# The sinks' products written first into the values' banks, and another order of work from step 7 on

## The chip, the cores and the metric

The kernel runs on one core of one Trainium2 chip. The metric is the device time of one launch in microseconds. Lower is better.

## What is computed

Attention over a window with sinks, and then a gated block. `q`, `k` and `v` have 4 batches, 8 heads, 768 positions and 64 features; a query sees the 4 first positions (the sinks) and the 128 positions that end at itself. The second part works on the heads put side by side (`x`: 4 x 768 x 512). Cut to what matters:

```
scores = scale * np.matmul(q, k.transpose(0, 1, 3, 2))
keep = is_sink | in_window                  # pos < 4, or 0 <= rel < 128
scores = np.where(keep, scores, -1000000000.0)
a = np.exp(scores - max); a = a / (np.sum(a) + 1e-09)
x = np.matmul(a, v)                         # then heads side by side
...
for k in range(5):                          # a causal convolution of 5 taps
    gate_pre += conv_w[k][None, None, :] * xp[:, k:k + S, :]
gate = 1.0 / (1.0 + np.exp(-gate_pre))
val = x @ w_val
out = gate * val @ w_out
```

All values are float32.

## The kernel before

**Steps and blocks.** The attention is cut into 24 steps: 4 batches, 3 parts of 256 positions, and 2 quads of 4 heads. Two steps (both quads of one part) make one of 12 blocks of the gated part. No loop runs on the chip: everything is laid out in one written order, the text `ORDER`. Its tokens are a short name and a step or block number, and each calls one function. Every engine, and each DMA queue, runs its own instructions in the order in which the tokens call them; semaphores hold an instruction until its inputs are there and its output's place is free.

**Tokens of a step (s is the step).** `kq.s` and `vv.s` load keys, queries and values through SP's queue. `s0.s` and `s1.s` are the scores of two halves of the quad (TensorE, L395), followed by a copy under a mask and a maximum on VectorE (L400, L404 or L409). `e0.s`, `e1.s` are the exponentials (ScalarE, L420), `rec.s` the reciprocal of the sums (L426, L427), `norm.s` the products with it on GpSimd (L435 to L443). `tx.s` turns the probabilities with sixteen transposes on TensorE (L455); `px.s` (VectorE, L486) and `py.s` (ScalarE, L494) take them out of PSUM, under the two masks. `sk.s` turns the sinks' probabilities (one transpose, L463), `ts.s` takes them out (L473). `vl.s` (`values`, L513) multiplies the turned probabilities with the values, 48 records in a step and 32 in a step of a batch's first part; `si.s` (`sinks`, L521) adds the sinks' part with two products. `sv.s` prepares the sinks' values (L260 on ScalarE, L263 twice on GpSimd).

**What follows a step.** The result of `vl` and `si` lies in the tile `xv`, two banks of PSUM, of which there is one copy. `xc.s` (L528) and `xh.s` (L536) copy it out on ScalarE, `hd.s` (L540) writes the four columns ahead of it for the convolution, `xl.s` (L544) and `c4.s` (L549) work on the copies on GpSimd, and `c0.s` and `c1.s` (L557, four instructions each on VectorE) read `xv` for the other four taps. The next step may write into `xv` only when all of them have read.

**Tokens of a block (m is the block).** `th` is the gate's tanh. `v0.m` to `v3.m` (L576) are the products with `w_val`, twelve matmuls each; `g0`, `g1` (L595) the gate on VectorE, `h0`, `h1` (L601) and `l0`, `l1` (L605) the split into a high and a low part on ScalarE and GpSimd; `o0.m` to `o3.m` (L629, in the last half L625) the products with `w_out`; `t0`, `t1` (L648, L638) take them out, `d0`, `d1` store them through SP's queue.

**Places in PSUM.** `pr` is two pairs of banks, which scores and transposes take in turn; `ac` (the list `homes`) is two single banks, taken by `sk`, by `v0` and `v2`, and by `o0` and `o2`, and put back by `ts`, by `g` and by `t`. `xv` is the last two.

**Forms of TensorE's array.** The products use four tilings of the array, shown in the profile as rows by columns: `128*128` (`v`, `o`, `sk`), `64*32` (`s`), `64*64` (`vl`) and `64*128` (`tx`, `si`).

Of the kernel before, what the change touches and what calls it, by code (L numbers as in the profile page):

```python
# [56 lines left out]
py.11 px.11 norm.12 xl.9 vv.13 vl.10 si.10 xc.10 hd.10 xh.10 kq.14 d1.3 tx.12 py.12 px.12 c4.10 c0.10 warm_up
v0.4 xl.10 v1.4 g0.4 d1.1 h0.4 l0.4 vv.11 c1.10 th.9 v2.4 e1.13 v3.4 g1.4 sk.11 ts.11 s1.14 s0.14 h1.4 vl.11
si.11 o0.4 sk.12 ts.12 e0.13 rec.13 l1.4 xc.11 hd.11 c4.11 sv.13 e0.14 norm.13 c0.11 o1.4 kq.18 e1.14 t0.4
c1.11 kq.15 o2.4 d0.3 o3.4 s0.18 s0.15 vv.12 th.11 xh.11 sv.12 vl.12 si.12 t1.4 xc.12 tx.13 rec.14 hd.12 xl.11  # L60
v0.5 c4.12 norm.14 xh.12 e0.15 px.13 c0.12 c1.12 v2.5 xl.12 v3.5 g1.5 py.13 th.10 v1.5 g0.5 h0.5 sk.13 ts.13
s1.15 h1.5 s1.18 d0.4 e1.15 vl.13 l0.5 si.13 o0.5 l1.5 xc.13 rec.15 hd.13 xh.13 s0.16 e0.16 th.12 tx.14 px.14
o2.5 kq.17 o1.5 t0.5 py.14 c4.13 c0.13 o3.5 t1.5 vv.14 e0.18 xl.13 vv.18 c1.13 s1.16 d1.5 sk.14 ts.14 norm.15
sk.15 ts.15 sv.18 vl.14 si.14 xc.14 hd.14 tx.15 px.15 e1.16 c4.14 c0.14 rec.16 py.15 norm.16 e1.18 c1.14 xh.14
v0.6 v1.6 g0.6 v2.6 h0.6 s0.17 vv.15 kq.19 s0.19 vl.15 si.15 rec.18 l0.6 th.13 vv.16 e0.17 xc.15 v3.6 g1.6
xl.14 c4.15 s1.17 hd.15 s1.19 th.14 h1.6 sk.16 ts.16 l1.6 xh.15 c0.15 xl.15 e1.17 rec.17 kq.20 e0.19 o0.6 o1.6
t0.6 tx.16 py.16 c1.15 px.16 v0.7 v1.7 norm.18 sk.18 ts.18 s0.20 d1.4 kq.21 e1.19 d0.6 vl.16 v2.7 e0.20 g0.7
h0.7 norm.17 l0.7 si.16 xc.16 c4.16 hd.16 tx.18 px.18 py.18 tx.17 v3.7 px.17 c0.16 o2.6 o3.6 th.15 g1.7 vv.23
rec.19 xh.16 c1.16 py.17 t1.6 s1.20 h1.7 xl.16 s0.21 e1.20 sk.17 ts.17 norm.19 o0.7 vv.17 th.16 rec.20 d0.5
l1.7 vl.17 si.17 xc.17 c4.17 hd.17 xh.17 e0.21 xl.17 norm.20 d1.6 c0.17 tx.19 py.19 o2.7 o3.7 o1.7 t0.7 c1.17  # L70
th.17 px.19 t1.7 kq.23 d1.7 s1.21 vl.18 d0.7 si.18 xc.18 c4.18 hd.18 vv.19 xh.18 e1.21 sv.19 tx.20 vv.20 px.20
c0.18 v2.8 xl.18 v3.8 g1.8 h1.8 kq.22 c1.18 th.18 v0.8 v1.8 sk.19 py.20 ts.19 g0.8 h0.8 vl.19 si.19 s1.22 l1.8
rec.21 s0.22 xc.19 hd.19 l0.8 xh.19 c4.19 xl.19 sk.20 o0.8 ts.20 o1.8 c0.19 c1.19 norm.21 e1.22 t0.8 d0.8 o2.8
e0.22 rec.22 v0.9 norm.22 th.19 tx.21 px.21 py.21 vl.20 si.20 vv.21 xc.20 c4.20 hd.20 xh.20 xl.20 s1.23 e1.23
s0.23 vv.22 v1.9 g0.9 h0.9 o3.8 t1.8 v2.9 e0.23 v3.9 l0.9 c0.20 c1.20 rec.23 sk.21 norm.23 ts.21 vl.21 si.21
xc.21 c4.21 g1.9 h1.9 l1.9 tx.22 py.22 px.22 tx.23 py.23 hd.21 xh.21 o2.9 xl.21 o0.9 o3.9 c0.21 o1.9 t1.9 t0.9
c1.21 px.23 th.20 sk.22 ts.22 vl.22 si.22 xc.22 c4.22 xh.22 xl.22 sk.23 ts.23 d1.9 hd.22 c0.22 c1.22 v0.10
v2.10 v1.10 th.22 g0.10 v3.10 h0.10 l0.10 vl.23 si.23 xc.23 c4.23 hd.23 xh.23 xl.23 th.21 flag g1.10 o0.10
o2.10 d1.8 c0.23 c1.23 v0.11 v1.11 th.23 g0.11 h0.11 l0.11 v2.11 d0.9 v3.11 g1.11 o0.11 h1.10 l1.10 h1.11
o1.10 l1.11 o1.11 t0.10 d0.10 t0.11 o3.10 t1.10 o2.11 d1.10 d0.11 o3.11 t1.11  # L80
# [809 lines left out]
```

## Time and profile before

| | |
|---|---|
| median of 3 runs | 263.9 us (263.66 to 264.38) |
| the profiled execution | 264.63 us |
| its span, first to last instruction | 262.8 us |
| granted clock of TensorE, mean | 0.997 |
| busy share PE, PEld, DVE, ACT, POOL | 97%, 78%, 78%, 72%, 67% |

PE is TensorE's matmuls, PEld its weight loads, DVE VectorE, ACT ScalarE, POOL GpSimd, SP the queue of DMAs. A busy share is over the whole span. The chain of waits follows the work that ended last back to its start; its pieces lie end to end, so that the length of a piece is what it added to the time.

### The profile page before, as it was taken

How to read it: one execution, taken by the hardware profiler on the slowest of the kernel's cores; microseconds unless marked ns; L12 is line 12 of the kernel's file. 1: busy time of each engine (PE TensorE's matmuls, PEld its weight loads, DVE VectorE, ACT ScalarE, POOL GpSimd, SP SyncE). 2: the span in 40 equal slices, each digit the busy share in tenths (PEclk: the TensorE clock that was granted, in tenths of full speed). 3: DMA queues.
4: the chain of work that ended last, by engine and by line, in shares of the span. 5: the costliest groups of instructions: out<-in, count | busy, mean ns of one | idle time of the engine just before them, and what ended most of it. 6: DMA issues, size and time to landing. Idle time of an engine off the chain costs nothing.

```text
span 262.8 us, 9921 instructions
## 1 busy us (share of the span) xinstructions
PE 253.6 (97%) x3960; PEld 205.5 (78%) x3964; DVE 204.7 (78%) x561; ACT 188.7 (72%) x692; POOL 177.4 (67%) x241
## 2 busy tenths in 40 slices
PE   7899989999999999999999999999999999999993
PEld 2355569779878878889879779889779788888982
DVE  5976999979979879997869698796878659667610
ACT  3899998979887677974796688986676768444231
POOL 6279897778668992878379665894782985933340
PEclk9999999999999999999999999999999999999998
DMA  6999382364323534755250529253407131030013
GB/s 201 379 340 341 113 262 74 109 168 144 106 78 118 183 131 146 218 171 180 63 174 2 161 81 326 78 185 111 142 4 231 68 106 59 2 122 0 2 44 128
DMA packets 27541, 36.45 MB, mean 139 GB/s; under 512 B 2272, under 2 KB 24032, under 8 KB 27488
## 3 DMA queue, kind: packets, MB, share of 16 engines
q1 hardware_dynamic: 26672, 34.96, 41.7%
q10 hardware_dynamic: 816, 0.79, 0.9%
q8 instruction: 33, 0.54, 0.9%
q14 instruction: 20, 0.16, 0.2%
HBM read 29.45 MB, written 6.29 MB: 136 GB/s over the span
## 4 chain that ended last, share of the span: by engine, by line
PE 79%; ACT 9%; POOL 4%; DMA 4%; DVE 1%; issue 1%; POOLq 0%
PE ac L576 24%; PE ac L629 22%; PE xv L513 11%; PE pr L395 9%; PE pr L455 4%; ACT w L420 4%; PE pr L629 3%; PE xv L521 2%; DMA raw<-in_w_val_dram 2%; DMA vs<-in_vsk_dram 2%; POOL xl L544 1%; PE ac L463 1%; POOL gl L605 1%; POOL vh L263 1%; ACT wv_p L140 1%
## 5 line engine op out<-in xcount | busy, mean ns | idle before, releaser
L557 DVE SCALAR_TENSOR_TENSOR sg<-xv,cw,sg 128x256 f32<-128x256 f32 x192 | 77.8, 474 | 3.3 <-POOL sg L549 2.9
L435 POOL TENSOR_TENSOR wx<-w,sm 128x512 f32<-128x512 f32 x48 | 49.2, 1047 | 5.7 <-DVE sm L427 4.0
L420 ACT ACTIVATE w<-pr,ngm 128x132 f32<-128x132 f32 x136 | 48.6, 370 | 1.6
L576 PE MATMUL ac<-xh,wvh 128*128 128x256 f32 x192 | 48.7, 288 | 0.0
L605 POOL TENSOR_TENSOR gl<-sg,gh 128x512 fp32r<-128x512 f32 x24 | 30.8, 1290 | 26.0 <-ACT gh L601 25.8
L576 PE MATMUL ac<-xh,wvl 128*128 128x256 f32 x192 | 47.0, 279 | 0.0
L549 POOL TENSOR_TENSOR sg<-xt,cw 128x512 f32<-128x512 f32 x24 | 25.5, 1063 | 17.9 <-ACT xt L528 16.5
L576 PEld LDWEIGHTS ac<-xh,wvh 128*128 128x128 f32 x192 | 36.2, 189 | 1.7 <-issue 0.5
L576 PEld LDWEIGHTS ac<-xh,wvl 128*128 128x128 f32 x192 | 36.1, 188 | 0.2
L395 PE MATMUL pr<-k,q 64*32 64x168 f32 x1536 | 35.0, 307 | 0.6 <-DVE wt L486 0.2
L513 PEld LDWEIGHTS xv<-wt,v 64*64 64x64 f32 x1024 | 30.3, 133 | 6.1 <-issue 2.6
L513 PE MATMUL xv<-wt,v 64*64 64x192 f32 (+2 forms) x1024 | 34.5, 278 | 0.2 <-ACT wt L494 0.2
L544 POOL TENSOR_TENSOR xl<-xt,xh 128x512 fp32r<-128x512 f32 x24 | 31.0, 1290 | 3.9 <-DVE sm L427 2.5
L629 PE MATMUL ac<-woh,gh 128*128 128x512 f32 x80 | 33.2, 415 | 0.0
L629 PE MATMUL ac<-woh,gl 128*128 128x512 f32 x80 | 31.8, 397 | 0.3 <-POOL gl L605 0.3
L629 PE MATMUL ac<-wol,gh 128*128 128x512 f32 x80 | 31.7, 396 | 0.0
L576 PE MATMUL ac<-xl,wvh 128*128 128x256 f32 x192 | 30.4, 280 | 0.1
L395 PEld LDWEIGHTS pr<-k,q 64*32 64x32 f32 x1536 | 24.0, 106 | 8.1 <-issue 2.1
L400 DVE COPY_PREDICATED pr<-low,pr 128x256 f32<-128x256 uint8 x48 | 20.3, 422 | 9.6 <-PE pr L395 4.9
L420 ACT ACTIVATION_READ_ACCUMULATOR w<-pr,ngm 128x1 f32 x136 | 27.6, 203 | 0.0
L576 PEld LDWEIGHTS ac<-xl,wvh 128*128 128x128 f32 x192 | 25.9, 188 | 0.3 <-POOL xl L544 0.3
L404 DVE TENSOR_REDUCE ngm<-pr 128x4 f32<-128x528 f32 x34 | 24.0, 707 | 1.2
(156 smaller groups left out, 480.0 us busy)
## 6 DMA issues: line engine op xcount, KB each, us to landing
k<-in_kt_dram SPq DMA_DIRECT2D x23, 408.0 KB, 4.1
...
```

Of the source, the lines that this page charges most:

```text
L395: nc.tensor.matmul(ss[e * QB:(e + 1) * QB, j, c * n + x0:c * n + x1], q[js, g, (4 * c + e) * QB:(4 * c + e + 1) * QB], k[js, g, (2 * c + e ...
L400: nc.vector.copy_predicated(sv[:, :, :, :D], low[:, None, None, :].to_broadcast([P, 2, 2, D]), sv[:, :, :, 2 * HB:])
L404: nc.vector.tensor_reduce(out=ngm[:, g], in_=sv[:, :, :, :PK], axis=mybir.AxisListType.X, op=ALU.max)
L420: nc.scalar.activation(out=w[:, g, j, c], in_=sx[:, j, c, :PK], func=AF.Exp, scale=0.125 if whole else -1.0, bias=ngm[:, g, j, c:c + 1], a ...
L435: nc.gpsimd.tensor_tensor(out=t[:, n].rearrange("p c h x -> p h c x"), in0=w[:, :, :, at], in1=sm.to_broadcast([P, 4, 2, D]), op=ALU.mult)
L513: nc.tensor.matmul(acc[o * D:(o + 1) * D, g, x0 + h * D:x0 + (h + a1 - a0 + 1) * D], v[js, g, n], t[js, n % 2, n // 2, g, a0:a1 + 1].rearr ...
L544: nc.gpsimd.tensor_tensor(out=half(xls, s, "xl", F32R), in0=xts[s], in1=half(xhs, s, "xh", F32R).bitcast(F32), op=ALU.subtract)
L549: nc.gpsimd.tensor_tensor(out=half(sg, s, "sg", F32), in0=xts[s], op=ALU.mult, in1=cw[:, g, KT - 1:].to_broadcast([P, 2, PQ]))
L557: nc.vector.scalar_tensor_tensor(out=g, in0=x, scalar=a, in1=g, op0=ALU.mult, op1=ALU.add)
L576: nc.tensor.matmul(acc[:, h], a[:, kc, cs], x[:, kc], start=(n == 0), stop=(n == 11))
L605: nc.gpsimd.tensor_tensor(out=gl, in0=g, in1=gh.bitcast(F32), op=ALU.subtract)
L629: nc.tensor.matmul(acc, a[:, kc, ts], x[:, kc], start=(kc + n == 0), stop=(kc + n == 5))
```

## The change

The 849 tokens stay the same; only their order differs, from the 219th on (`s0.7` before, `y1.1` after). A constant `SIF = 8` is added: from step 8 on `sinks` opens the accumulation in the banks of `xv` (`start=True`) and `values` adds to it and closes it, so that `si.s` can stand ahead of `vl.s`. No instruction is added or removed, and no size is changed. The two functions and the first lines of the order:

```diff
 e1.5 kq.8 c0.3 scalars d0.0 py.4 rec.5 v0.1 v1.1 y0.1 c1.3 e1.6 rec.6 v2.1 norm.5 g0.1 th.3 h0.1 v3.1 vv.4
-s0.7 l0.1 vl.4 y1.1 g1.1 e0.7 h1.1 l1.1 s1.7 s1.8 o2.1 si.4 e1.7 tx.5 xc.4 xh.4 px.5 hd.4 c4.4 c0.4 c1.4 o3.1
-t1.1 o0.1 e1.8 py.5 kq.9 sk.5 ts.5 norm.6 o1.1 t0.1 tx.6 py.6 rec.7 vl.5 si.5 xc.5 xl.4 px.6 c4.5 sk.6 ts.6
-hd.5 xh.5 xl.5 s0.9 s0.8 th.4 norm.7 v0.2 v1.2 e0.9 c0.5 tx.7 c1.5 e0.8 rec.8 norm.8 v2.2 py.7 px.7 g0.2 h0.2
-s1.9 kq.10 s1.10 vl.6 l0.2 si.6 xc.6 c4.6 th.5 sk.7 ts.7 hd.6 d0.1 vv.7 v3.2 xh.6 sv.7 o2.2 g1.2 c0.6 o0.2
-h1.2 c1.6 e1.9 rec.9 l1.2 o3.2 e1.10 d1.0 t1.2 tx.8 xl.6 px.8 py.8 vl.7 si.7 xc.7 hd.7 xh.7 sk.8 norm.9 ts.8
-c4.7 s0.10 tx.9 th.6 px.9 c0.7 d1.11 c1.7 o1.2 t0.2 e0.10 rec.10 xl.7 v0.3 vv.8 py.9 v1.3 vv.9 g0.3 h0.3 kq.12
...
+y1.1 vl.4 tx.5 d1.0 kq.9 si.4 g1.1 l0.1 px.5 s1.8 sk.5 hd.4 xc.4 ts.5 o0.1 h1.1 c4.4 o2.1 xh.4 c0.4 warm_up
+c1.4 py.5 l1.1 e1.8 o3.1 t1.1 s0.7 s1.7 vl.5 xl.4 norm.6 kq.10 tx.6 e0.7 si.5 sk.6 py.6 px.6 ts.6 xc.5 xh.5
+o1.1 hd.5 e1.7 xl.5 s0.9 rec.7 t0.1 s0.8 v0.2 c4.5 c0.5 v1.2 th.4 kq.12 g0.2 v2.2 c1.5 e0.9 norm.7 e0.8 rec.8
+sk.7 h0.2 v3.2 l0.2 norm.8 tx.7 ts.7 th.5 g1.2 vl.6 py.7 si.6 px.7 hd.6 h1.2 xc.6 c4.6 l1.2 xh.6 xl.6 s1.9
+s1.10 vv.7 c0.6 c1.6 o2.2 o0.2 vv.8 sv.7 e1.9 e1.10 o3.2 tx.8 rec.9 px.8 s0.12 vl.7 norm.9 kq.18 py.8 t1.2
+si.7 xc.7 c4.7 s0.10 tx.9 d0.1 sk.8 hd.7 xh.7 xl.7 ts.8 th.6 c0.7 kq.11 e0.12 e0.10 o1.2 d1.2 v0.3 px.9 c1.7
+vv.9 v1.3 g0.3 s1.12 py.9 t0.2 s0.11 rec.10 si.8 vl.8 xc.8 s1.11 kq.13 xh.8 h0.3 hd.8 d0.2 sk.9 c4.8 ts.9 l0.3
...
@@ -88,6 +88,7 @@
 MP = 10
 LAST = (B * NP - 1, 1)
 COPIES = 2
+SIF = 8
@@ -497,11 +498,15 @@
     xhs, xls, sg, accs = {}, {}, {}, {}
+    def summed(s):
+        if s not in accs:
+            bank = ps_v.tile([P, 2, 512], F32, name="xv", tag="xv")
+            accs[s] = bank[:, :, :KT - 1 + PQ]
+        return accs[s]
+
     def values(s):
         b, p, qd = steps[s]
-        v, t, x0 = vv[s], probs[s], KT - 1
-        bank = ps_v.tile([P, 2, 512], F32, name="xv", tag="xv")
-        accs[s] = acc = bank[:, :, :KT - 1 + PQ]
+        v, t, x0, acc = vv[s], probs[s], KT - 1, summed(s)
         tiles = [(g, j, j if g == 0 else 1 - j) for g in range(2) for j in range(2)]
         n0 = 2 if p == 0 else 0
@@ -512,14 +517,14 @@
                 h = n - 2 + a0
                 nc.tensor.matmul(acc[o * D:(o + 1) * D, g, x0 + h * D:x0 + (h + a1 - a0 + 1) * D], v[js, g, n],
                                  t[js, n % 2, n // 2, g, a0:a1 + 1].rearrange("p a r -> p (a r)"),
-                                 start=(n == n0), stop=False, skip_group_check=True)
+                                 start=(n == n0 and s < SIF), stop=(n == 5 and s >= SIF), skip_group_check=True)
     def sinks(s):
         b, p, qd = steps[s]
         for g in range(2):
             gs = slice(g * D, (g + 1) * D)
-            nc.tensor.matmul(accs[s][:, g, KT - 1:], vs[b, qd][gs], skt[s][gs].rearrange("p c r -> p (c r)"),
-                             start=False, stop=True, skip_group_check=True)
+            nc.tensor.matmul(summed(s)[:, g, KT - 1:], vs[b, qd][gs], skt[s][gs].rearrange("p c r -> p (c r)"),
+                             start=(s >= SIF), stop=(s < SIF), skip_group_check=True)
     xts = {}
```

The tokens that issue work on TensorE, from `v0.1` to the end, with | where the form of the array changes. Before:

```
v0.1 v1.1 v2.1 v3.1 | s0.7 | vl.4 | s1.7 s1.8 | o2.1 | si.4 tx.5 | o3.1 o0.1 sk.5 o1.1 | tx.6 | vl.5 | si.5 | sk.6 |
s0.9 s0.8 | v0.2 v1.2 | tx.7 | v2.2 | s1.9 s1.10 | vl.6 | si.6 | sk.7 v3.2 o2.2 o0.2 o3.2 | tx.8 | vl.7 | si.7 | sk.8
| s0.10 | tx.9 | o1.2 v0.3 v1.3 | s0.12 s0.11 | vl.8 | si.8 | s1.11 | sk.9 v2.3 v3.3 o2.3 | s1.12 s1.13 | vl.9 | si.9
tx.10 | o3.3 o0.3 o1.3 sk.10 | s0.13 | tx.11 | vl.10 | si.10 tx.12 | v0.4 v1.4 v2.4 v3.4 sk.11 | s1.14 s0.14 | vl.11 |
si.11 | o0.4 sk.12 o1.4 o2.4 o3.4 | s0.18 s0.15 | vl.12 | si.12 tx.13 | v0.5 v2.5 v3.5 v1.5 sk.13 | s1.15 s1.18 |
vl.13 | si.13 | o0.5 | s0.16 | tx.14 | o2.5 o1.5 o3.5 | s1.16 | sk.14 sk.15 | vl.14 | si.14 tx.15 | v0.6 v1.6 v2.6 |
s0.17 s0.19 | vl.15 | si.15 | v3.6 | s1.17 s1.19 | sk.16 o0.6 o1.6 | tx.16 | v0.7 v1.7 sk.18 | s0.20 | vl.16 | v2.7 |
si.16 tx.18 tx.17 | v3.7 o2.6 o3.6 | s1.20 s0.21 | sk.17 o0.7 | vl.17 | si.17 tx.19 | o2.7 o3.7 o1.7 | s1.21 | vl.18 |
si.18 tx.20 | v2.8 v3.8 v0.8 v1.8 sk.19 | vl.19 | si.19 | s1.22 s0.22 | sk.20 o0.8 o1.8 o2.8 v0.9 | tx.21 | vl.20 |
si.20 | s1.23 s0.23 | v1.9 o3.8 v2.9 v3.9 sk.21 | vl.21 | si.21 tx.22 tx.23 | o2.9 o0.9 o3.9 o1.9 sk.22 | vl.22 |
si.22 | sk.23 v0.10 v2.10 v1.10 v3.10 | vl.23 | si.23 | o0.10 o2.10 v0.11 v1.11 v2.11 v3.11 o0.11 o1.10 o1.11 o3.10
o2.11 o3.11
```

After:

```
v0.1 v1.1 v2.1 v3.1 | vl.4 | tx.5 si.4 | s1.8 | sk.5 o0.1 o2.1 o3.1 | s0.7 s1.7 | vl.5 | tx.6 si.5 | sk.6 o1.1 | s0.9
s0.8 | v0.2 v1.2 v2.2 sk.7 v3.2 | tx.7 | vl.6 | si.6 | s1.9 s1.10 | o2.2 o0.2 o3.2 | tx.8 | s0.12 | vl.7 | si.7 |
s0.10 | tx.9 | sk.8 o1.2 v0.3 v1.3 | s1.12 s0.11 | si.8 | vl.8 | s1.11 | sk.9 v2.3 v3.3 o2.3 | s1.13 | tx.10 si.9 |
vl.9 | sk.10 o3.3 o0.3 o1.3 | s1.18 | tx.11 si.10 | vl.10 | s0.18 s0.13 | sk.11 v0.4 v1.4 v2.4 v3.4 | tx.12 si.11 |
vl.11 | s1.14 s0.14 | sk.12 o2.4 o3.4 o0.4 o1.4 | tx.13 si.12 | vl.12 | s1.15 s0.15 | v0.5 v1.5 v2.5 sk.13 v3.5 |
tx.14 si.13 | s1.16 | vl.13 | sk.14 o2.5 o3.5 | s0.16 s0.17 | o0.5 o1.5 | tx.15 si.14 | vl.14 | v0.6 sk.15 v1.6 v2.6
v3.6 sk.16 | s0.19 | tx.16 si.15 | vl.15 | s1.17 s1.19 | o0.6 o1.6 v0.7 v1.7 | tx.17 tx.18 si.16 | vl.16 | o2.6 sk.17
o3.6 v2.7 v3.7 | s1.20 s0.20 | si.17 | sk.18 o0.7 | vl.17 | s0.21 | o1.7 o2.7 sk.19 o3.7 | tx.19 tx.20 si.18 | vl.18 |
s1.21 | v2.8 v0.8 v3.8 v1.8 | si.19 | vl.19 | s1.22 s0.22 | sk.20 o0.8 o1.8 v0.9 v1.9 | tx.21 si.20 | vl.20 | s0.23
s1.23 | sk.21 o2.8 o3.8 v2.9 v3.9 | tx.22 si.21 | vl.21 | sk.22 o0.9 o2.9 o3.9 o1.9 | tx.23 si.22 | vl.22 | sk.23
v0.10 v2.10 v1.10 v3.10 | si.23 | vl.23 | o0.10 o2.10 v0.11 v2.11 v1.11 v3.11 o1.10 o0.11 o1.11 o3.10 o2.11 o3.11
```

Of the other tokens the prediction speaks of these: `norm.8` stands ahead of `l0.2` and `c4.6` before, and behind `l0.2` but still ahead of `c4.6` after; `vv.19` behind `t1.7` and `d0.7` before, right behind `vv.16` and ahead of `s1.19` after; `flag` (eight small instructions on VectorE) between `th.21` and `g1.10` before, between `c1.21` and `ts.23` after; `warm_up` (one small instruction on ScalarE) behind `c0.10` before, behind `c0.4` after.

## Rows read from the trace of the kernel before

**Rows 1.** Windows: us, busy (instructions) by engine PE, PEld, DVE, ACT, POOL, clock, DMA.

```profile
81.00:204.00 123.00, 123.00 (x2076) 104.76 (x2074) 102.91 (x284) 90.87 (x353) 86.31 (x117) 1.00 0.45 141
...
209.30:258.30 49.00, 48.96 (x561) 43.38 (x559) 29.19 (x70) 23.34 (x69) 26.09 (x30) 1.00 0.17 56
258.30:262.80 4.50, 0.00 (x0) 0.00 (x0) 0.00 (x0) 0.38 (x1) 0.00 (x0) 0.84 0.22 71
```

**Rows 2.** The chain of waits: start us, us, engine, output, line, records.

```profile
58.85 5.80 PE ac L576 x48
64.65 0.73 PE pr L395 x32
...
66.86 1.30 PE pr L395 x64
68.16 1.60 PE ac L629 x6
69.76 0.32 PE xv L521 x2
70.08 0.50 PE pr L455 x16
...
73.58 0.11 PE ac L463
...
75.08 0.64 PE pr L455 x16
75.72 1.48 PE xv L513 x48
...
137.71 1.14 PE xv L513 x32
...
198.54 4.16 DMA vs<-in_vsk_dram
...
233.58 0.26 PE ac L463
```

**Rows 3.** PE's timeline at three places: start us, us, instruction, [idle before].

```profile
44.35 0.63 PE L576 MATMUL ac<-xl,wvh 128*128 128x256 f32 x4
...
80.05 1.03 PE L576 MATMUL ac<-xl,wvh 128*128 128x256 f32 x4
...
205.17 0.39 PE L521 MATMUL xv<-skt,vh 64*128 64x256 f32 x2
205.66 1.38 PE L395 MATMUL pr<-k,q 64*32 64x168 f32 x64
...
207.36 0.40 PE L629 MATMUL ac<-wol,gh 128*128 128x512 f32 x1
208.04 0.50 PE L629 MATMUL ac<-woh,gl 128*128 128x512 f32 x1 [0.28 <-POOL gl L605]
```

**Rows 4.** VectorE's timeline: a convolution, a gate, the flag's first and last instruction.

```profile
80.78 3.22 DVE L557 SCALAR_TENSOR_TENSOR sg<-xv,cw,sg 128x256 f32<-128x256 f32 x8
...
84.93 0.68 DVE L595 SCALAR_TENSOR_TENSOR sg<-sg,ac 128x512 f32<-128x512 f32 x1
...
239.18 0.16 DVE L109 CAST nw_f<-nw_raw 128x4 f32<-128x4 int32 x1
...
241.33 0.15 DVE L120 CAST flag_i<-flag 128x1 int32<-128x1 f32 x1
```

**Rows 5.** GpSimd's timeline around steps 6 and 8.

```profile
84.25 2.05 POOL L435 TENSOR_TENSOR wx<-w,sm 128x512 f32<-128x512 f32 x2 [0.81 <-DVE sm L427]
...
87.16 1.29 POOL L605 TENSOR_TENSOR gl<-sg,gh 128x512 fp32r<-128x512 f32 x1
88.40 1.06 POOL L549 TENSOR_TENSOR sg<-xt,cw 128x512 f32<-128x512 f32 x1
```

**Rows 6.** Groups of the page: line, shapes, count, busy us, mean ns, idle before.

```profile
L486 DVE TENSOR_TENSOR wt<-pr,cur 128x512 f32<-128x512 f32 x24 | 16.3, 678 | 9.4 <-PE pr L455 5.2 <-ACT wt L494 4.1
...
L494 ACT ACTIVATE wt<-pr 128x256 f32<-128x256 f32 x40 | 13.6, 387 | 3.4 <-DVE wt L486 2.5 <-PE pr L455 0.9
```

More of the change, by code (lines that the diff above doesn't have):

```diff
@@ L52 @@
-h1.2 c1.6 e1.9 rec.9 l1.2 o3.2 e1.10 d1.0 t1.2 tx.8 xl.6 px.8 py.8 vl.7 si.7 xc.7 hd.7 xh.7 sk.8 norm.9 ts.8
-c4.7 s0.10 tx.9 th.6 px.9 c0.7 d1.11 c1.7 o1.2 t0.2 e0.10 rec.10 xl.7 v0.3 vv.8 py.9 v1.3 vv.9 g0.3 h0.3 kq.12
-s0.12 kq.11 s0.11 th.7 d1.2 l0.3 vl.8 si.8 xc.8 hd.8 c4.8 xh.8 d0.2 s1.11 sk.9 e0.11 norm.10 ts.9 xl.8 v2.3
-e1.11 v3.3 c0.8 c1.8 g1.3 e0.12 h1.3 o2.3 s1.12 l1.3 kq.13 s1.13 rec.11 e1.12 rec.12 vl.9 si.9 xc.9 th.8 c4.9
-hd.9 xh.9 tx.10 px.10 kq.16 py.10 o3.3 t1.3 vv.10 norm.11 o0.3 o1.3 t0.3 c0.9 c1.9 sk.10 ts.10 s0.13 tx.11
@@ L57 @@
[L57 to L80, printed above, removed]
+y1.1 vl.4 tx.5 d1.0 kq.9 si.4 g1.1 l0.1 px.5 s1.8 sk.5 hd.4 xc.4 ts.5 o0.1 h1.1 c4.4 o2.1 xh.4 c0.4 warm_up
@@ new lines @@
+vv.9 v1.3 g0.3 s1.12 py.9 t0.2 s0.11 rec.10 si.8 vl.8 xc.8 s1.11 kq.13 xh.8 h0.3 hd.8 d0.2 sk.9 c4.8 ts.9 l0.3
+th.7 c0.8 c1.8 e0.11 norm.10 v2.3 v3.3 o2.3 vv.10 g1.3 s1.13 e1.11 tx.10 si.9 vl.9 px.10 h1.3 e1.12 rec.11
+xc.9 l1.3 sk.10 xh.9 hd.9 ts.10 o3.3 c4.9 c0.9 py.10 norm.11 d1.1 kq.14 c1.9 o0.3 o1.3 e1.13 s1.18 tx.11 xl.9
+t1.3 py.11 si.10 t0.3 px.11 vl.10 th.8 xc.10 rec.12 e1.18 d1.3 s0.18 s0.13 xl.8 vv.13 vv.12 vv.11 sk.11 th.9
+v0.4 v1.4 ts.11 hd.10 v2.4 xh.10 d1.11 e0.18 v3.4 e0.13 c4.10 c0.10 c1.10 norm.12 kq.17 sv.13 kq.16 sv.12
@@ new lines @@
+tx.12 si.11 vl.11 py.12 g0.4 h0.4 g1.4 h1.4 hd.11 px.12 l0.4 s1.14 s0.14 sk.12 l1.4 xc.11 ts.12 rec.13 c4.11
+c0.11 kq.15 e1.14 o2.4 o3.4 o0.4 norm.13 c1.11 e0.14 t1.4 th.10 o1.4 xl.10 tx.13 xh.11 si.12 px.13 t0.4 th.11
+rec.14 py.13 vl.12 vv.18 xl.11 hd.12 xc.12 s1.15 c4.12 s0.15 xh.12 c0.12 xl.12 v0.5 v1.5 v2.5 d0.4 g0.5
+norm.14 e1.15 sk.13 e0.15 vv.15 c1.12 v3.5 ts.13 g1.5 h0.5 tx.14 si.13 px.14 h1.5 s1.16 l0.5 py.14 vl.13
+rec.15 hd.13 sk.14 l1.5 d1.4 xc.13 ts.14 c4.13 xh.13 o2.5 c0.13 o3.5 norm.15 s0.16 c1.13 xl.13 e1.16 s0.17
@@ new lines @@
+o0.5 o1.5 vv.14 e0.16 tx.15 t0.5 si.14 t1.5 th.12 vl.14 v0.6 px.15 rec.16 xc.14 hd.14 th.13 sk.15 ts.15 d0.5
+v1.6 py.15 c4.14 v2.6 c0.14 e0.17 rec.18 v3.6 g0.6 norm.16 sk.16 c1.14 h0.6 kq.19 g1.6 norm.18 xh.14 h1.6
+s0.19 kq.22 tx.16 l0.6 py.16 si.15 px.16 vl.15 xc.15 xl.14 s1.17 vv.16 vv.19 d1.5 s1.19 xh.15 ts.16 hd.15 o0.6
+l1.6 e1.17 rec.17 o1.6 c4.15 xl.15 e1.19 c0.15 v0.7 v1.7 c1.15 e0.19 norm.17 tx.17 th.14 t0.6 tx.18 si.16
+vl.16 kq.20 g0.7 px.18 sv.19 o2.6 px.17 sk.17 xc.16 py.18 c4.16 ts.17 o3.6 rec.19 hd.16 sv.18 c0.16 norm.19
@@ new lines @@
+xh.16 h0.7 v2.7 c1.16 py.17 v3.7 d0.3 th.15 g1.7 t1.6 s1.20 l0.7 s0.20 h1.7 e1.20 si.17 vv.17 sk.18 l1.7 xl.16
+e0.20 ts.18 kq.21 o0.7 vl.17 xc.17 xh.17 s0.21 o1.7 rec.20 c4.17 hd.17 t0.7 e0.21 o2.7 d0.7 c0.17 sk.19 o3.7
+vv.20 c1.17 tx.19 ts.19 norm.20 py.19 t1.7 tx.20 xl.17 si.18 vl.18 px.19 s1.21 th.16 xc.18 c4.18 th.17 xh.18
+hd.18 vv.21 c0.18 v2.8 c1.18 v0.8 v3.8 v1.8 e1.21 px.20 xl.18 si.19 g0.8 g1.8 th.18 py.20 vl.19 h0.8 l0.8 h1.8
+rec.21 xc.19 kq.23 s1.22 xh.19 l1.8 c4.19 s0.22 xl.19 d0.6 hd.19 e0.22 sk.20 o0.8 d1.7 ts.20 o1.8 v0.9 v1.9
@@ new lines @@
+c0.19 norm.21 e1.22 c1.19 tx.21 si.20 vl.20 px.21 rec.22 g0.9 t0.8 s0.23 py.21 s1.23 xc.20 c4.20 sk.21 norm.22
+xh.20 ts.21 hd.20 o2.8 th.19 o3.8 c0.20 v2.9 v3.9 c1.20 vv.22 g1.9 e0.23 e1.23 tx.22 h0.9 t1.8 h1.9 si.21
+xl.20 vl.21 l0.9 sk.22 py.22 xc.21 hd.21 ts.22 l1.9 px.22 o0.9 c4.21 rec.23 xh.21 o2.9 norm.23 o3.9 d1.8 xl.21
+o1.9 tx.23 c0.21 th.20 vv.23 d0.8 t0.9 t1.9 c1.21 py.23 si.22 vl.22 xc.22 sk.23 flag hd.22 xh.22 ts.23 v0.10
+px.23 c4.22 c0.22 v2.10 v1.10 c1.22 g0.10 v3.10 d1.6 h0.10 th.21 th.22 l0.10 xl.22 si.23 vl.23 o0.10 g1.10
@@ L81 @@
+xh.23 xc.23 xl.23 hd.23 d0.9 h1.10 c4.23 c0.23 c1.23 o2.10 l1.10 v0.11 v2.11 v1.11 v3.11 th.23 g0.11 h0.11
+o1.10 g1.11 d1.9 h1.11 l0.11 o0.11 l1.11 t0.10 o1.11 o3.10 t0.11 d0.10 t1.10 d0.11 d1.10 o2.11 o3.11 t1.11
 """
```

## The prediction

> **What bounds the kernel now.** I read the windows first. From 81 to 204 us TensorE (PE) is busy without a gap, 123.00 of 123.00 us, and from 209.3 to 258.3 in 48.96 of 49.00, at the full clock; VectorE, the next, is busy in 102.91 of the 123. Only the last 4.50 us hold no matmul [rows 1]. A busy PE may still wait inside its pipeline, so I went on to the chain of waits. From 58.85 us on, nearly every piece of it is PE's, end to end, and the pieces repeat to 0.01 us: a piece's length depends on what it computes and on whether its neighbours use the same form of the array. The time therefore is a sum of PE pieces and a few stalls, and a new order is priced by laying the same pieces in the new order.
>
> The prices [rows 2]: four `v` in a row, with other forms on both sides, take 5.80, one `o` 1.60. So a `v` or `o` takes (5.80 - 1.60) / 3 = 1.40, and a stretch of the `128*128` form, however long, 0.20 for coming and going. A `tx` alone takes 0.64, an `si` alone 0.32, but an `si` followed by a `tx` 0.32 + 0.50: two of the `64*128` form side by side save 0.14. Scores take 0.73 alone and 1.30 as a pair, 0.16 less than two alone. Values take 1.48, or 1.14 in a batch's first part, whatever stands beside them. An `sk` inside or at the end of a `128*128` stretch takes 0.11; alone it takes 0.26, which is 0.06 beside the stretch's 0.20, and I price one at the head of a stretch at 0.06 too.
>
> Three stalls are on top, read from PE's timeline [rows 3]. In `v0.2` the four products with the low part take 1.03 in place of 0.63: 0.40. Behind `si.19` the next scores start 0.49 after it in place of 0.32: 0.17. In `o0.8` the product with `gl` starts 0.68 after the one before it, against 1.40 / 6 = 0.23, and its own start-up costs some 0.1 again: 0.55. Together 1.1 us. What lies behind the last two is the load of `vs`, 4.16 us on the chain [rows 2], with `sv.19` and then the block's low parts queued behind it on GpSimd.
>
> **The change part by part: fewer changes of form.** From `v0.1` to the end I counted the stretches in the two lists of TensorE's tokens. `128*128` stretches go from 31 to 24: 7 x 0.20 = -1.40. `64*128` stretches go from 28 to 23, since from step 9 on most `tx` now stand beside an `si`: 5 x 0.14 = -0.70. Stretches of scores go from 21 to 22: +0.16. Stretches of values stay 20. Of the 19 `sk`, 7 at a head, 2 alone and 10 inside or at an end become 13 at a head and 6 inside or at an end: four times 0.06 - 0.11 = -0.20. In sum -2.14 us.
>
> Two orders are rare or new in the trace: `si` directly ahead of `vl`, and `tx` ahead of `si`. The nearest rows are `tx` (the same form as `si`) ahead of `vl`, 0.64 and then 1.48, each its usual length [rows 2]. I take the usual prices; the bounds are nothing and 0.10 (half of what a `128*128` stretch pays) for each of the 16 steps.
>
> A rule can be weighed here. The Trainium skill, "TensorEngine Tiling (Array Packing)", section Key Properties, says that a change of tiling mode drains TensorE; "TensorE: Matmul & The Clock Gate", Part 2, gives the drain as some 128 cycles, an estimated 53 ns at 2.4 GHz. There are 11 changes fewer, so by these figures the gain would be 0.6 us and not 2.1; the rows, which show 0.14 to 0.20 for each stretch, decide.
>
> **The old stalls.** They should go. `v0.2` follows the last write of step 5 into `xv` after 2.96 us of PE work instead of 1.56 (in between stand `sk.6 o1.1` and the scores of 9 and 8), so `xl.5` is ready. `vv.19`, which carries `vs`, is issued ahead of `s1.19` in place of behind `t1.7` and `d0.7`; its values are wanted some 35 us of PE work later. -1.1 us; kept whole, it would be 0.
>
> **The new waits.** I laid the pieces of the new order end to end from 58.85 and held the other engines' queues against them. The first place: `sk.7` now stands inside `v0.2 v1.2 v2.2 sk.7 v3.2` and takes the bank of `ac` that `g0.2` frees. PE reaches it at 83.0. `c0.5` starts on VectorE at 80.8, as before, since `s0.8` and `rec.7` still stand ahead of it; half of 3.22 and 0.68 later [rows 4] `g0.2` ends at 83.1, and with the signal I take 0.2. The second: `s0.10` takes the pair of banks of `tx.8`, because `s0.12` was moved in between, so it waits for `py.8`. `c1.5` and `rec.8` end at 84.9, `l0.2` at 86.2, then `norm.8` (2.9), now behind it, and `c4.6` (1.06) end at 90.2 [rows 5]; `c0.6` and `c1.6` at 93.4 [rows 4], `rec.9` at 93.6, `px.8`, two of 678 ns, at 94.9 and `py.8`, two of 387 ns, at 95.6 [rows 6], against 95.2 on PE's clock (95.4 with the first stall): 0.3. The third, by the same reckoning: `s0.13` waits for `px.11`, 0.2. Behind it I find margins of 0.3 us and more, and put in 0.15 for what I overlook: +0.85. The bounds are 0 and 2.0: ten places take a bank of `ac` only one piece of 1.40 after its reader could start, and each may be 0.2 late (before there are eight such, and none shows a stall).
>
> **At nothing.** The flags of accumulation change no instruction's size. `flag` (241.48 - 239.18 = 2.3 us of VectorE [rows 4]) moves to a place where VectorE waits for `sk.23`: with that cover gone, `ts.23` and with it `v2.10` would be up to 1 us late. `warm_up` is one small instruction. SP's queue: every load but `kq.11` is issued at least 7 us ahead of its use; `kq.11` has 5.7 us. The tail behind the last matmul stays 4.50.
>
> **Sum.** -2.14 - 1.1 + 0.85 = -2.4 us. The profiled execution took 264.63 around its span of 262.8, so it would take 262.2; the runs' median is 0.7 lower, 263.9, so the time is **261.5 us**. A measurement here tells some 0.3% (0.8 us) from no change.
>
> **Rivals.** *The sinks wait for the convolution (slower).* `si.s`, now first, may not write before `c1.(s-1)` has read `xv`. Summed over PE's pieces, from the last write into `xv` to the next step's first it is 7.3 us on average before and 7.1 after (steps 8 to 23), the shortest 5.71 and 5.74; the convolution alone is 3.22 of it [rows 4], and a copy and `c4` go ahead. If VectorE came late by 0.21 at each of the 16 sinks, the whole 3.3 us would be gone; from 0.26 on the kernel is slower, at 0.3 it takes 265.4. Against it: `vl` paid no such wait before, at nearly the same distance. Chance 0.06.
>
> *Waits eat it (no change).* The new order's handovers of `ac` and `pr` banks stall PE 2.5 to 4.1 us in all: 263.1 to 264.7, at their middle 263.9. It needs the 2.0 of my bound and more. Chance 0.10.
>
> *The change of forms saves less.* If `si` ahead of `vl` paid 0.10 at each of the 16 steps, 1.6 of the gain would go: 263.1. The rows speak against it: `vl` takes 1.48 behind a `tx` too [rows 2]. Chance 0.08, about half of it on the faster side of 263.1. (The drain that the Trainium skill gives, in the two sections above, as the only price of a change, would put the sum at -0.6 - 1.1 + 0.85 = -0.85, an estimated 263.05; it is counted in this chance, and no row here shows so small a price.)
>
> **How the numbers follow.** My forecast has 0.76. With no new stall at all the lowest run (263.66) would come to 260.4; with stalls of 2.0 the median comes to 262.7 and the highest run to 263.1. I give 260.4 to 263.0; what lies outside is most of the last three cases. Faster is 0.76 + 0.04 + 0.03 (stalls just short of 2.5 in the second case, where its bounds are soft) = 0.83, the same 0.04 + 0.07 = 0.11, slower 0.06.
>
> **What would show it.** In the new profile the chain should again be PE's from some 60 us on, with `tx` and `si` pieces of 0.82 together, `128*128` stretches of 1.40 a piece and 0.20, and values of 1.48 behind `si`. PE's last matmul should end 2.4 us earlier, near 255.9. No chain piece should be a DMA of `vs`, and the stalls should stand at `sk.7`, `s0.10` and `s0.13`. It is wrong if `vl` or `si` are longer beside each other, if PE shows waits for L557 ahead of L521, or if a load comes late, `kq.11` first.

## The result, and the profile after

The changed kernel takes 261.24 us (median of 6 runs, 260.89 to 261.67) against 263.94 (6 runs, 263.66 to 264.44) for the kernel before: a ratio of 0.9892, 95% interval 0.9880 to 0.9904, 2.7 us less. Forecast were 261.5 us and a range of 260.4 to 263.0. A second set of runs, taken beside experiments, gave 261.31 and a ratio of 0.9895 (0.9877 to 0.9913).

| | before | after |
|---|---|---|
| the profiled execution | 264.63 us | 260.89 us |
| its span | 262.8 us | 259.1 us |
| PE, from the start of `v0.1` to the start of `o2.11` | 196.47 us | 193.70 us |
| the same in the second set's profile | | 193.88 us |

The two profiled spans differ by more than the medians. The third line is the better measure: it holds the whole part that is in another order and leaves out the start and the tail, which are the same in both and vary from one execution to the next. (`v0.1` begins at 58.24 to 58.78 in the eleven profiles of this study.) Of that stretch 2.78 us went, 2.60 in the second profile. All "by the profile" figures below are of this stretch.

The windows of the changed kernel (us, then busy time by engine as in [rows 1]) show PE as full as before:

```profile
81.00:200.00 119.00, 119.00 (x2052) 101.05 (x2052) 100.51 (x280) 88.53 (x350) 86.21 (x117) 1.00 0.46 145
200.00:253.50 53.50, 53.50 (x670) 47.03 (x669) 34.82 (x82) 27.66 (x83) 29.86 (x33) 1.00 0.19 61
```

So the gain isn't idle time that shows in a window. It must be in the lengths of PE's pieces. The chain of waits of the changed kernel, with the columns of [rows 2]; lines 395, 455, 463, 513, 521, 576 and 629 of before are now 396, 456, 464, 518, 526, 581 and 634:

```profile
58.47 5.80 PE ac L581 x48
64.27 1.48 PE xv L518 x48
...
109.75 0.64 PE pr L456 x16
110.39 0.17 PE xv L526 x2
110.56 1.48 PE xv L518 x48
...
119.52 1.38 PE pr L396 x64
...
166.89 1.38 PE pr L396 x64
...
195.22 0.78 PE pr L396 x32
...
212.71 1.36 PE pr L396 x64
```

The prices are those of before: 5.80 for four `v`, 0.64 for `tx`. A `tx` and the `si` behind it take 0.64 + 0.17 = 0.81, and the `vl` behind them its usual 1.48, although it now follows a sink that has opened the sum. The last four lines are scores that take 0.05 to 0.08 more than the 0.73 alone or 1.30 as a pair of [rows 2]: they come back in the account of the waits below. No piece of the chain from 58 us on is a transfer of `vs`. PE's last matmul ends at 255.11 on the chain, where it was 258.27: 3.16 earlier, of which 0.39 is the earlier start of `v0.1`.

PE's timeline at the three places where I had put new stalls, `sk.7`, `s0.10` and `s0.13`, and where the two late stalls of [rows 3] stood (columns as there):

```profile
82.34 0.40 PE L581 MATMUL ac<-xl,wvh 128*128 128x256 f32 x2
82.57 0.27 PE L464 MATMUL ac<-ident,skb 128*128 128x128 f32 x1
...
94.50 0.38 PE L526 MATMUL xv<-skt,vh 64*128 64x256 f32 x2
94.82 0.81 PE L396 MATMUL pr<-k,q 64*32 64x168 f32 x32
...
119.45 1.45 PE L396 MATMUL pr<-k,q 64*32 64x168 f32 x64
...
203.19 1.37 PE L396 MATMUL pr<-k,q 64*32 64x168 f32 x64
...
204.89 0.39 PE L634 MATMUL ac<-wol,gh 128*128 128x512 f32 x1
205.12 0.39 PE L634 MATMUL ac<-woh,gl 128*128 128x512 f32 x1
```

`sk.7` (82.57) follows the last of `v2.2` at the usual distance. `s0.10` (94.82) starts 0.32 after its sink, the usual length of a sink. The pair that ends with `s0.13` takes 1.45 in place of 1.37 or 1.38. The last two lines are `o0.8`: its product with `gl` starts 0.23 after the one before it, where it was 0.68. The two new stalls at the front are near misses. VectorE's timeline shows the first:

```profile
79.50 0.71 DVE L405 TENSOR_REDUCE ngm<-pr 128x4 f32<-128x528 f32 x1
80.13 1.65 DVE L562 SCALAR_TENSOR_TENSOR sg<-xv,cw,sg 128x256 f32<-128x256 f32 x4
81.70 0.68 DVE L600 SCALAR_TENSOR_TENSOR sg<-sg,ac 128x512 f32<-128x512 f32 x1
```

`g0.2` (L600) frees the bank at 82.37, 0.2 before `sk.7` takes it. `c0.5` (L562) started at 80.13, where I had let it start at 80.8, "as before" [rows 4]: it follows the scores `s0.8`, and these came 0.7 earlier too (77.55 on PE in place of 78.30). Of these 0.7 us, 0.39 is the earlier start of `v0.1` in this execution, by which PE comes to `sk.7` earlier as well; 0.3 is the new order. `py.8` ended at 94.77, 0.05 before `s0.10`; I had 95.6, of which 0.39 is again the start and 0.4 the order.

The second set's profile has one wait more, at `s0.11`. The pair of scores that ends with it took 1.58 there and 1.37 in the first profile; the line of SP is the issue of the `q` of `kq.11`:

```profile
96.09 1.07 SPq L242 DMA_DIRECT2D q<-in_qt_dram  x1
...
100.61 1.58 PE L396 MATMUL pr<-k,q 64*32 64x168 f32 x64
```

This `q` landed at 101.14, and PE started `s0.11` at 101.39, where 101.21 was its turn. In the first profile it was issued at 96.14 and landed at 100.86, and `s0.11` started on its turn, at 101.26. So in one of two executions the load of `kq.11` was late, by 0.19.

### The profile page after: what moved, and what is told of

It is laid out like the page before. It is cut to its first block, busy times and chain, and to the rows that moved or that the text cites. A ratio compares the mean times of both kernels' runs of the same rounds, so it can differ in the third digit from the quotient of the medians.

```text
span 259.1 us, 9951 instructions
## 1 busy us (share of the span) xinstructions
PE 251.7 (97%) x3960; PEld 204.2 (79%) x3964; DVE 205.0 (79%) x561; ACT 187.1 (72%) x692; POOL 176.9 (68%) x241
## 4 chain that ended last, share of the span: by engine, by line
PE 84%; ACT 9%; DMA 2%; POOL 2%; DVE 1%; issue 1%
PE ac L581 26%; PE ac L634 22%; PE xv L518 12%; PE pr L396 10%; PE pr L456 5%; ACT w L421 4%; PE pr L634 3%; DMA raw<-in_w_val_dram 2%; PE xv L526 2%; PE ac L464 2%; ACT wv_p L141 1%; ACT wv_p L160 1%; ACT wvl L187 1%; PE ac L630 1%; PE pr L630 1%
## 5 line engine op out<-in xcount | busy, mean ns | idle before, releaser
L562 DVE SCALAR_TENSOR_TENSOR sg<-xv,cw,sg 128x256 f32<-128x256 f32 x192 | 77.8, 473 | 6.9 <-POOL sg L554 6.0
L549 POOL TENSOR_TENSOR xl<-xt,xh 128x512 fp32r<-128x512 f32 x24 | 30.8, 1287 | 3.8 <-ACT xh L541 2.6
```

The lines of the kernel that those rows point to most:

```text
L549: nc.gpsimd.tensor_tensor(out=half(xls, s, "xl", F32R), in0=xts[s], in1=half(xhs, s, "xh", F32R).bitcast(F32), op=ALU.subtract)
L562: nc.vector.scalar_tensor_tensor(out=g, in0=x, scalar=a, in1=g, op0=ALU.mult, op1=ALU.add)
```

## The experiments

Each ran beside the kernel before on the same chip (before: 264.02 in the first set, 264.13 in the second, 264.07 in the third; 16 to 23 runs each). The diffs are of the list of tokens, cut to what moves.

### The two halves of the change, each without the other

`e2_sinks_last`, the new order with the sinks where they were:

```diff
-SIF = 8
+SIF = 24
 for every s from 8 to 23:
-si.s vl.s        (or si.s some tokens ahead of vl.s)
+vl.s si.s
```

> The new order with one thing undone: each sinks' product from step 8 on stands directly behind its values again and closes the sum, and the values start it. Theory (pieces by form): the 64*128 stretches go from 23 to 35, since every sink now stands alone between values and another form; 12 x 0.14 = 1.7 us more, and nothing else changes, so 261.2 + 1.7 or 1.8 = 263.0 us (262.6 to 263.4), with si pieces of 0.32 where they now take 0.17 behind a tx. First rival (the gain came from the order of scores, v and o alone; a sink costs the same anywhere): 261.2. Second rival (sinks first made the values wait for the convolution, so undoing it frees PE): under 261.

Measured: 262.77 us (262.47 to 263.42), ratio to before 0.9954 (0.9938 to 0.9970). That is 1.46 more than the changed kernel on the same chip (261.31), and still 1.25 less than before. The chain of waits at the same place as above:

```profile
110.00 0.64 PE pr L456 x16
110.64 1.48 PE xv L518 x48
112.12 0.32 PE xv L526 x2
```

`tx` and `vl` have their lengths; the sink takes 0.32 behind the values against 0.17 behind `tx`. Measured from one piece's start to the next one's, over all of them, the `tx` are 1.45 us longer than in the changed kernel and the `si` 0.29: 1.74 / 12 = 0.145 for each stretch, the price of the forecast. Values and scores are 0.29 shorter together (0.51 against the second profile): small waits of the changed kernel are not there with the sinks last. So 1.46 is the price of twelve stretches less those waits. The theory holds. The first rival falls. So does the second: 0.3 to 0.5 us of waiting did go, but nearly all of it ahead of scores, which write to other banks than the convolution reads.

The Trainium skill, "TensorEngine Tiling (Array Packing)", section Key Properties, has a change of form drain the engine, and by the some 128 cycles that "TensorE: Matmul & The Clock Gate", Part 2, gives for a matmul's last column to leave the array, the 12 stretches would cost an estimated 0.64 us. The pieces show 1.74. That a change of form costs time agrees with the trace; the estimate is too small.

`e1_sinks_first_alone`, the old order with the sinks first:

```diff
-SIF = (none; values start, sinks close)
+SIF = 8
 for every s from 8 to 23:
-vl.s si.s
+si.s vl.s
```

> The old order, and only the sinks' part of the change: from step 8 on each si stands directly ahead of its vl, starts the sum, and the values close it. Theory (pieces by form): by pieces it is 0.86 us longer than before, since the old order had six sinks beside a tx that now stand alone (34 stretches of 64*128 in place of 28, 6 x 0.14); and at steps 10, 11, 13, 14, 19, 21 and 22 an si now follows its sk within one piece, so PE waits for the transposed copy of the sums, some 0.3 to 0.8 us each time: 266 to 269 us, slower than before. First rival (sinks first is what saves time, whatever the order): some 2 us faster than before, 262. Second rival (the flags and the place of the sink cost nothing): 263.9.

Measured: 269.61 us (269.38 to 269.76), ratio 1.0201 (1.0179 to 1.0223): 5.5 us slower than before. From the table of PE's waits (us in total, times, longest):

```profile
PE xv L526 <- DVE skt L474: 4.2, 5, 1.4
```

PE's timeline at step 14:

```profile
157.32 0.44 PE L464 MATMUL ac<-ident,skb 128*128 128x128 f32 x2
159.12 0.39 PE L526 MATMUL xv<-skt,vh 64*128 64x256 f32 x2 [1.37 <-DVE skt L474]
```

The old order has `sk.14` right ahead of `vl.14`: the values gave VectorE 1.48 us to turn the sums (`ts.14`) before the sink wanted them. With the sink first that cover is gone, and PE stands still at five such places, 1.4 us at the longest: at steps 14, 19, 21 and 22 of the theory's list, and at 17, which is not on it. At 10, 11 and 13 no sink waits, and `si.12` waits for something else, its values on GpSimd (`sv.12`, L264). So the theory's mechanism holds, but not its places and lengths, and the time lies 0.6 above its range. So the two halves are not worth anything like their sum: the sinks moved alone cost 5.5 us, the order alone gives 1.25, both together 2.7. The new order has `sk.s` a whole stretch of `v` and `o` ahead of `si.s`, and no sink waits for its sums there. I take that distance to be what makes the sink's new place free; no run took it away alone.

### What a stretch costs

`e5_sinks_scores_apart`, the new order with six `sk` set apart:

```diff
-sk.9 c4.8 ts.9 l0.3 ...                  (behind s1.11)
+sk.9 s1.11 ...                           (ahead of s1.11)
-tx.10 si.9 vl.9 ... sk.10 ... o3.3
+tx.10 si.9 sk.10 vl.9 ... o3.3
 and in the same way
+sk.14 vl.13    sk.21 s0.23    sk.22 vl.21    sk.23 vl.22
```

> The new order with six sk (9, 10, 14, 21, 22, 23) moved by a few tokens, so that each stands alone between two other forms in place of at the head of a 128*128 stretch. The work is the same, instruction for instruction. Theory (a 128*128 stretch costs 0.20 for coming and going): 30 stretches in place of 24, 6 x 0.20 = 1.2 us more: 262.4 us (262.1 to 262.8), with pieces of 0.26 for these sk, and no new wait. First rival (a change of form costs only a drain of some 0.05): 6 x 0.05 = 0.3 us more, 261.5, which cannot be told from no change. Second rival (the moved sk wait for their banks): more than 0.3 us longer at one or two of the six places, and the others as before.

Measured: 262.90 us (262.64 to 263.22), ratio 0.9954 (0.9938 to 0.9971): 1.59 more than the changed kernel. The chain of waits at `sk.9` and `sk.10`:

```profile
103.78 0.26 PE ac L464
104.03 0.73 PE pr L396 x32
104.77 3.00 PE ac L581 x24
...
110.71 0.26 PE ac L464
```

PE's timeline at `sk.21`:

```profile
213.82 0.30 PE L464 MATMUL ac<-ident,skb 128*128 128x128 f32 x1 [0.56 <-DVE sg L600]
```

An `sk` alone takes 0.26, and the stretch that it left still pays its own 0.20: 3.00 for `v2.3 v3.3`. From one piece's start to the next one's, `sk.9`, `sk.10` and `sk.14` went from 0.085 to 0.258, and the piece that now opens their old stretch is 0.02 to 0.03 longer: 0.19 to 0.20 each. PE also stands still ahead of the other three: 0.63 at `sk.21`, by the profile for the gate (L600) that reads its bank, 0.20 at `sk.22` and 0.03 at `sk.23`. So the theory's price holds, but not its "no new wait": the second rival comes on top of it at one or two places, and the time lies 0.1 above the theory's range. In the pieces it is 1.1 us of stretches and 0.9 of waits, of which 0.1 to 0.3 come back in the scores. The first rival, 0.3 us, falls.

### The three old stalls

`e3_vs_early`, the old order with two loads changed about:

```diff
-vv.23 rec.19 ... hd.18 vv.19 xh.18 e1.21 sv.19
+vv.19 rec.19 ... hd.18 vv.23 xh.18 e1.21 sv.19
```

> The old order, in which the loads vv.19 and vv.23 change places, so that the block's vs is asked for some ten steps of the list earlier; nothing else. Theory: the stalls behind si.19 (0.17) and in o0.8 (0.55) go, as the load of vs and sv.19 behind it are what is late: 0.7 us less than before, 263.2 (262.9 to 263.5), and the chain holds no transfer of vs. Rival (those stalls come from the order around them, not from the load): 263.9, stalls where they were.

Measured: 263.87 us (263.29 to 264.59), ratio 0.9986 (0.9972 to 1.0000): 0.26 less, where 0.7 was expected. By the profile 0.39. PE's timeline:

```profile
204.86 0.39 PE L521 MATMUL xv<-skt,vh 64*128 64x256 f32 x2
205.49 0.91 PE L395 MATMUL pr<-k,q 64*32 64x168 f32 x35 [0.24 <-DMA q<-in_qt_dram]
...
207.19 0.40 PE L629 MATMUL ac<-wol,gh 128*128 128x512 f32 x1
207.43 0.40 PE L629 MATMUL ac<-woh,gl 128*128 128x512 f32 x1
```

`o0.8` is mended (0.24 from `wol` to `gl`), so that stall was the load of `vs` with `sv.19` behind it. The one behind `si.19` is longer than before, 0.63 in place of 0.49, and the profile names its end: the transfer of `q` of step 22. In the kernel before SP issued that load at 201.17, and it took 4.4 us to land: 205.52, and `s1.22` started at 205.66. I had read the wrong load.

`e7_vs_and_q_early` tests that reading:

```diff
 as in the run before, and
-... xh.16 ... kq.22 c1.18 th.18
+... hd.18 kq.22 vv.23 xh.18 ... c1.18 th.18
```

> The old order with vv.19 and vv.23 changed about as in the run before, and kq.22 put ahead of them, so that the q of step 22 is asked for earlier too; nothing else. Theory (formed on the run before, where the stall behind si.19 stayed and the transfer of q was named as its end): the 0.17 behind si.19 and the 0.55 in o0.8 both go, 263.3 us (263.0 to 263.6), some 0.7 under before, and scores start 0.32 after si.19. First rival (the stall behind si.19 is VectorE's or ScalarE's reading of the pair of banks): it stays, 263.9. Second rival (another load is late in their place, that of vv.23 or kq.23): 263.9 or more.

Measured: 263.19 us (262.80 to 263.75), ratio 0.9971 (0.9956 to 0.9986): 0.88 less than before, by the profile 0.73. Both stalls are gone:

```profile
204.62 0.39 PE L521 MATMUL xv<-skt,vh 64*128 64x256 f32 x2
204.94 1.37 PE L395 MATMUL pr<-k,q 64*32 64x168 f32 x64
...
206.64 0.39 PE L629 MATMUL ac<-wol,gh 128*128 128x512 f32 x1
206.87 0.40 PE L629 MATMUL ac<-woh,gl 128*128 128x512 f32 x1
```

So each of the two late stalls had a load of its own, and both loads stood in one queue. The changed kernel issues `q` of step 22 at 196.2 and `vs` far ahead; that is why both went there.

`e4_no_old_stalls` is the run with `vv` changed about, and the low part of step 5 put on GpSimd's queue earlier:

```diff
-si.5 xc.5 xl.4 px.6 c4.5 sk.6 ts.6 hd.5 xh.5 xl.5 s0.9
+si.5 xl.4 xc.5 xh.5 xl.5 c4.5 hd.5 px.6 sk.6 ts.6 s0.9
```

> The run before with one thing more: behind si.5, xl.5 is put on its queue before the scores of step 9 and the low part of the v before it, so that v0.2 has its low part in time. Theory: the three stalls of the old order (1.1 us) go, nothing else: 262.8 (262.5 to 263.2), and the rest of the way to the changed kernel (1.6 us) is forms. Rival (v0.2's four products with the low part are long for another reason, or xl.5 ahead delays the chain): no gain over the run before, 263.2 or more.

Measured: 263.85 us (263.72 to 264.28), ratio 0.9988 (0.9977 to 0.9999), the same as without it. PE's timeline:

```profile
79.75 0.63 PE L576 MATMUL ac<-xl,wvh 128*128 128x256 f32 x4
...
81.77 0.46 PE L455 MATMUL pr<-ident,wx 64*128 64x64 f32 x8
82.77 0.46 PE L455 MATMUL pr<-ident,wx 64*128 64x64 f32 x8 [0.54 <-POOL wx L435]
```

GpSimd's timeline:

```profile
79.67 1.05 POOL L549 TENSOR_TENSOR sg<-xt,cw 128x512 f32<-128x512 f32 x1
80.67 2.05 POOL L435 TENSOR_TENSOR wx<-w,sm 128x512 f32<-128x512 f32 x2
```

`v0.2` is mended: the four products with the low part take 0.63 in place of the 1.03 of [rows 3]. But `tx.7`, which comes 0.4 earlier, now wants `norm.7` (L435) while GpSimd is still at it, and the second half of it waits. So putting `xl.5` ahead of `c4.5` (L549) is enough to mend `v0.2`, but not to save time: GpSimd is late for what comes next as well.

`e8_v2_ahead_of_tx7` adds PE work ahead of `tx.7`, to the loads of `e7` and the queue of `e4`:

```diff
-v0.2 v1.2 e0.9 c0.5 tx.7 c1.5 ... v2.2 py.7 px.7 g0.2 ... s1.9 s1.10 vl.6 ... sk.7 ts.7 ... v3.2
+v0.2 v1.2 e0.9 c0.5 g0.2 v2.2 v3.2 sk.7 tx.7 c1.5 ts.7 ... py.7 px.7 ... s1.9 s1.10 vl.6
```

> The kernel of the run beside it, and with it the stall in v0.2 taken on again: xl.5 goes on its queue right behind si.5, as in the earlier run in which tx.7 then waited for the normalised rows, and v2.2, v3.2 and sk.7 now stand ahead of tx.7, so that PE has work while they are made. Theory: v0.2 takes its usual time (-0.40), tx.7 does not wait, and one 128*128 stretch fewer (-0.15 with the place of sk.7): 0.55 under the run beside it, 262.8 us (262.4 to 263.1). Rival (GpSimd is behind in this stretch whatever PE's order, so the wait only moves on to sk.7, tx.7 or vl.6): no gain over the run beside it, 263.3 or more.

Measured: 265.26 us (264.92 to 267.29), ratio 1.0054 (1.0033 to 1.0074): slower than before. `v0.2` and `tx.7` wait for nothing, but the table of PE's waits has new ones:

```profile
PE pr L395 <- ACT gh L601: 1.0, 1, 1.0
...
PE ac L629 <- POOL gl L605: 0.5, 1, 0.5
PE ac L629 <- DVE sg L595: 0.3, 1, 0.3
```

The first is `s1.10`, which takes the pair of banks of `tx.7` with only `s1.9` between, and started at 87.06. ScalarE's `h0.2` (L601), which the table names, had been done by 86.43; what ended last was `px.7` on VectorE, at 86.96, which empties that pair. In the new order `vl.6` and `si.6` stand between `tx.7` and the scores. So the rival's number holds, 263.3 or more, but not its mechanism: the longest wait is for VectorE's emptying of a pair of banks and not for GpSimd, and `sk.7`, `tx.7` and `vl.6` don't wait. Neither of the two moves tried in this stretch gains anything alone.

### Going further

`e6_sinks_first_from_6` carries the sinks' part two steps on:

```diff
-SIF = 8
+SIF = 6
-tx.7 ts.7 ... vl.6 py.7 si.6
+tx.7 si.6 ts.7 ... vl.6 py.7
-tx.8 ... s0.12 vl.7 ... si.7 ... s0.10 tx.9
+tx.8 si.7 ... vl.7 s0.12 ... s0.10 tx.9
```

> The change carried two steps further: the sinks go first from step 6 on, si.6 and si.7 directly behind tx.7 and tx.8, and the scores s0.12 move down to stand beside s0.10. Theory: two 64*128 stretches fewer (2 x 0.14) and one lone group of scores fewer (0.16): 0.45 us less than the changed kernel, 260.8 us (260.5 to 261.2). Rival (the early sinks are not ready, or the values of steps 6 and 7 wait for the convolutions of 5 and 6): 0.3 to 1 us of waiting, 261.1 to 261.8.

Measured: 262.20 us (262.09 to 262.33), ratio 0.9932 (0.9915 to 0.9950): 0.89 more than the changed kernel. PE's timeline:

```profile
84.26 0.71 PE L456 MATMUL pr<-ident,wx 64*128 64x64 f32 x16
84.78 0.36 PE L526 MATMUL xv<-skt,vh 64*128 64x256 f32 x2
85.07 1.21 PE L518 MATMUL xv<-wt,v 64*64 64x192 f32 x32
...
92.69 0.60 PE L526 MATMUL xv<-skt,vh 64*128 64x256 f32 x2
...
94.36 1.37 PE L396 MATMUL pr<-k,q 64*32 64x168 f32 x64
96.83 0.37 PE L456 MATMUL pr<-ident,wx 64*128 64x64 f32 x5 [1.10 <-DVE ngm L410]
```

At step 6 it works: `tx` and `si` take 0.81, and `vl.6` follows at once. At step 7 `si.7` comes 0.25 late and is 0.24 longer. The convolution that reads its bank, `c1.6`, had ended at 92.54, 0.15 before the first of its two products, so the 0.25 is the forecast's slower rival in small. The second product started at 92.90: it waited for the second instruction of `sv.7` on GpSimd, which ended at 92.85. So both halves of this run's rival are there, the sink that is not ready and the convolution:

```profile
91.88 0.97 POOL L264 TENSOR_TENSOR vh<-vs,vh 16x128 fp32r<-16x128 f32 x2
```

The larger loss, 1.1 us, is in no expectation, and with it the time lies above the rival's range too: `s0.12`, moved down to form a pair, is emptied by VectorE until 96.7, and `tx.9` takes its pair of banks. There are only two pairs of `pr` banks, so a pair of scores can delay whoever comes second behind it. What is left of the idea, `si.6` alone, would be worth 0.14, less than these runs can tell; I didn't run it.

`after_again`, the changed kernel as it is:

> The changed kernel again, on the same chip as the three experiments, as their measure: 261.2 us (260.9 to 261.6).

Measured: 261.31 us (261.01 to 261.44).

## Why the prediction was right, point by point

The time came out 0.3 us under the forecast, within its own range, and by the mechanism that it named: PE's pieces laid end to end. Of the three terms one held in size, one held with a wrong reason, and one was mis-sized.

- **Fewer changes of form, -2.14.** Held, by its parts: 0.82 predicted for `tx` and `si`, 0.81 measured; `vl` 1.48 behind a sink, so the bound of 0.10 a step did not come in; 0.145 for a `64*128` stretch over twelve places, where the term has 0.14; 0.19 to 0.20 for a `128*128` stretch at three places, where it has 0.20. That the whole is 2.14 is the sum of these prices; no run took away all of it and nothing else. A sum over all pieces agrees: if each piece between the starts of `v0.1` and `o2.11` is given the median length that it has between the same forms in the eleven profiles, the new list is 2.10 shorter than the old.
- **The old stalls, -1.1.** All three are gone. The step that failed is a sentence of the reading: "What lies behind the last two is the load of `vs`". It holds for `o0.8` (mended with `vs` early); the stall behind `si.19` was `q` of step 22, queued behind that load on SP and landing at 205.52. The two loads together are worth 0.73 by the profile and 0.88 by the times. The stall in `v0.2` went too: in the changed kernel `xl.5` ends at 78.11, and the first product that wants it starts at 79.30. The forecast gave one reason, the PE work put in between. There is a second, which it did not name: the new list also has `xl.5` ahead of `c4.5` on GpSimd, where `c4.5` (78.23 to 79.27) stood in front of it before, and by `e4` that alone is enough to mend `v0.2`. No run has the PE work without it. In the old order neither of two runs had it alone: the wait moved to `tx.7`, and then to `s1.10`.
- **The new waits, +0.85.** Mis-sized. At `sk.7` and `s0.10` PE waits for nothing, and the pair with `s0.13` is 0.08 longer (1.38 on the chain in place of 1.30); the other waits that I find are 0.08 at the pair with `s1.19`, 0.05 at `s1.21` and 0.06 at the pair with `s1.23`: 0.27 together. The second profile has 0.19 more at `s0.11`. The step that failed is that I laid PE's pieces on a new clock but left VectorE's `c0.5` at its old time, 80.8. An engine that is fed by PE comes earlier with it: counted from the start of `v0.1`, `c0.5` came 0.3 and `py.8` 0.4 ahead of my reckoning. That these were near misses (0.2 and 0.05 us) shows that the places were the right ones to look at.
- **The sum.** -2.4 forecast, -2.70 measured by the medians. With the waits that I found in place of the 0.85 it would be -2.14 - 1.1 + 0.27 = -3.0, and -2.8 for the second execution; the profiles show -2.78 and -2.60. The 0.2 that is left is spread over pieces that differ by 0.01 to 0.03, and I can't assign it. So the sum came out closer than its terms, and that much of it is luck: the waits were put 0.6 too high, and the 0.2 that no term has went the other way.
- **The signs of being wrong.** No sink waited for a convolution from step 8 on, and PE shows no wait at `v2.10`, where `flag` might have brought one. The load of `kq.11`, which the prediction named first among those that could come late, was in time in the first profile and 0.19 late in the second. The time lies near the lower third of the range, whose lower end was no new stall at all.

The rival that the change saves less because sinks first cost something was the right one to fear, but for another reason than I gave: not what `vl` pays behind `si`, but the distance from `sk.s` to `si.s`. The forecast didn't price that distance. In the old order it would have decided the sign.
